# Query loads with token pairs woven for the block turn, and one decode step more at the entry of the late stage

## The chip, the cores and the metric

The kernel runs on one core of one Trainium2 chip. The time is device microseconds of one execution of the program on that core. The engines are named as the profile names them: PE (TensorE), PEld (its weight loads), DVE (VectorE), ACT (ScalarE), POOL (GpSimd) and SP (SyncE, which here issues nearly all DMAs).

## What is computed

Linear attention with random features over 4 batches, 8 heads, 576 tokens and head size 64, then two gated or plain feed-forward layers over the 2304 tokens, all in float32:

```python
def phi(x):                                   # x: q or k, scaled by 64 ** -0.25
    proj = np.einsum('bhsd,md->bhsm', x, omega)          # 128 features
    h = proj - np.sum(x * x, axis=-1, keepdims=True) / 2.0
    return np.exp(h - np.max(h, axis=-1, keepdims=True)) / np.sqrt(m)
kv = np.einsum('bhsm,bhsd->bhmd', k_p, v);  z = np.sum(k_p, axis=2)
num = np.einsum('bhsm,bhmd->bhsd', q_p, kv)
out = num / (np.einsum('bhsm,bhm->bhs', q_p, z)[..., None] + 1e-06)
# x: out as 2304 tokens x 512
xn = x / sqrt(mean(x * x) + 1e-06) * rms_g;  g = xn @ w_gate          # 512 x 1536
x = (silu(g) * (xn @ w_val)) @ w_out                                   # 1536 x 512
h = x @ w_in;  out = silu(h) @ w_out2                                  # 512 x 2048, 2048 x 512
```

The weights arrive as float64 and are decoded on the chip from their two 32-bit words.

## The kernel before

Every float32 product of the feed-forward layers is three passes over a high and a low part (`PASS`). The program has two stages.

**The attention stage** is a list of operations (`Op`), each with an engine, a duration, the operations it needs, the buffers it claims and frees. A table written out by hand, `ORDER`, gives the sequence in which all of them are emitted, and so the order on each engine; every engine runs its own list in order. `run_order` walks that table with the durations written in the `Op`s and with `LAT`, `TURN` and `LAND`, and uses the resulting clock for one thing alone: which of a resource's slots (`SLOTS`; six PSUM buffers `b`, four tiles `x`, four `e`, two `qT` and so on) an operation gets, the one that is free first by this reckoning.

A unit is 256 tokens of four heads of q or k (kinds `q`, `k`), or the 64 tokens that are left over in each of two batches (`qt`, `kt`). For a unit, SP loads a tile `x` (L530; the left-over ones L521), POOL squares it (L581), PE turns it (L632), PE projects it on the features (L661, into a PSUM buffer `b`), DVE takes maxima (L678) and ACT the exponentials `e` (L709). From k, PE adds the products with v (L739, `kv`); the left-over tokens' v lies in the tile `vat` (L521). From q, the exponentials must be turned so that the features lie on the partitions, and then PE multiplies them with `kv` (L843). That turn is done in two ways. For units 0 to 17 of a running count (`count`, `BY_DMA`) PE turns (L819) and ACT copies (L825). For the 18 others, those of the last two batches and one pair of left-over pieces, SP moves four blocks of 32 partitions from `e` to `qT` (L799, four DMAs, operation `ed`) and DVE turns 32 x 32 blocks back into `e` (L806, operation `eT`). Then DVE divides (L857 to L877), ACT, POOL and PE normalise and turn the result into `xs`, the input of the layers (L908 to L961). In the gaps PE computes the first sweep of the first layer for the first three of five blocks of tokens (L250 and L1067).

In this stage all DMAs go through SP's one list, in the order of the table: loads of q, k, v and weights, and the moves `ed`. An x load is written as

```python
nc.sync.dma_start(out=dst.rearrange("p h r d -> p h (r d)"),
    in_=src[b, heads, 256 * hf:256 * hf + 256, :].rearrange("h (p r) d -> p h (r d)", r=2))
```

so partition p holds tokens 2p and 2p+1 (`r`), 512 bytes together for each head. The turn of `e` writes its 128 tokens at every fourth element (`p h (t b) -> p b h t`).

**The late stage** begins with `run_order`'s end. A generator, `stream`, issues the remaining sweeps of both layers on PE without a gap by intent (L250 the first products `g`, L304 and L337 the second products `y`), in PSUM buffers that take over the place of the six `b`. Between them, `prep.tick` moves a pipeline of weights on by one step: it emits the decode of one weight on DVE (L154 to L165) and POOL (L168), the scale and the high part of the one before on ACT (L176, L191), the low part of the one before that on DVE (L194), and the load of one more (L142, L144). A tick is emitted whenever `due`, a count of PE time, passes 3.2 or 5.5.

Of the kernel before, what the change touches and what calls it, by code (L numbers as in the profile page):

```python
# [20 lines left out]
def kernel(  # L21
# [14 lines left out]
    nc = tc.nc  # L36
# [6 lines left out]
    G = 4  # L43
    KC = DM // P
# [61 lines left out]
    f = 0  # L106
# [4 lines left out]
    f = 0  # L111
# [121 lines left out]
    prep = Prep()  # L233
# [5 lines left out]
    W_EARLY, GRAIN, GATE = 3, 3, 3  # L239
# [155 lines left out]

    ops = []
    LAT = {"PE": 0.22, "DVE": 0.15, "ACT": 0.18, "Pool": 0.08, "SP": 0.0}
    PE_SLOW, TURN, LAND = 5.5, 0.1, 2.4
    FIRST = {"PE": 1.5, "DVE": 2.0, "ACT": 3.3, "Pool": 2.4, "SP": 0.7}


# [112 lines left out]
    va_ring = [kp.tile([P, G, 2, D + 1], F32, tag=f"va{n}", name=f"va{n}", bufs=1) for n in range(SLOTS["v"])]  # L514
    va_tail = [kp.tile([P, G, 1, D + 1], F32, tag=f"vat{n}", name=f"vat{n}", bufs=1) for n in range(2)]

    def fetch(dst, src, kind, b, hf, g, parts=range(2)):
        heads = slice(G * g, G * g + G)
        if len(kind) == 2:
            for e in parts:  # L520
                nc.sync.dma_start(  # L521
                    out=dst[64 * e:64 * e + 64, :, 0, 0:D],
                    in_=src[b + e, heads, 512:576, :].rearrange("h p d -> p h d"),
                )
        elif src is v:
            rows = src[b, heads, 256 * hf:256 * hf + 256, :].rearrange("h (p r) d -> p h r d", r=2)
            for r in range(2):
                nc.sync.dma_start(out=dst[:, :, r, 0:D], in_=rows[:, :, r, :])
        else:
            nc.sync.dma_start(  # L530
                out=dst.rearrange("p h r d -> p h (r d)"),
                in_=src[b, heads, 256 * hf:256 * hf + 256, :].rearrange(
                    "h (p r) d -> p h (r d)", r=2
                ),
            )
# [27 lines left out]
    count, BY_DMA = [0], range(18, 36)  # L563

    def add_load(u):
        kind, b, hf, g = u
        tail = len(kind) == 2
        R = 1 if tail else 2
        w = ld[u] = State()

        def emit(o):
            w.x = buf(load_p, [P, G, R, D], "x", o.slot["x"])
            fetch(w.x, k if kind[0] == "k" else q, *u)

        w.op = Op("ld_x." + kind[0], "SP", 1.2 if tail else 0.5, emit, claim=["x"], xfer=0.55 * R)

        def squares(o):
            w.sq = buf(wk, [P, G * R * D], "sq", o.slot["sq"])
            w.ns = buf(wk, [P, G * R], "ns", o.slot["ns"])
            xf = w.x.rearrange("p h r d -> p (h r d)")  # L580
            nc.gpsimd.tensor_tensor(out=w.sq, in0=xf, in1=xf, op=ALU.mult)  # L581

        def halve(n):
            sv = w.sq.rearrange("p (a d) -> p a d", d=D)
            nc.gpsimd.tensor_tensor(  # L585
                out=sv[:, :, 0:n], in0=sv[:, :, 0:n], in1=sv[:, :, n:2 * n], op=ALU.add
            )

        w.sqop = Op("sq." + kind[0], "Pool", 0.17 + 0.43 * R, squares, [w.op], ["sq", "ns"])
        h1 = Op("half1." + kind[0], "Pool", 0.17 + 0.28 * R, lambda o: halve(D // 2), [w.sqop])  # L590
        h2 = Op("half2." + kind[0], "Pool", 0.17 + 0.14 * R, lambda o: halve(D // 4), [h1])

        def norms(o):
            nc.vector.tensor_reduce(  # L594
                out=w.ns, in_=w.sq.rearrange("p (a d) -> p a d", d=D)[:, :, 0:D // 4], axis=AX.X, op=ALU.add
            )

        w.nsop = Op("norms." + kind[0], "DVE", 0.2, norms, [h2], free=[(w.sqop, "sq")])
        if kind == "k":
            z = vld[u] = State()  # L600

            def emit_v(o):
                z.v = va_ring[o.slot["v"]]
                fetch(z.v, v, *u)

            z.op = Op("ld_v", "SP", 1.0, emit_v, claim=["v"], xfer=1.7)
        return w
# [12 lines left out]
    def add_unit(u):  # L620
        kind, b, hf, g = u
        tail = len(kind) == 2
        R = 1 if tail else 2
        w = add_load(u)
        st = State()
# [68 lines left out]
            [top], free=[(w.sqop, "ns")],  # L694
        )
        res = f"et{g}" if kind == "kt" else "e"
        base = count[0]
        if kind[0] == "q":
            count[0] += R
        moved = lambda r: kind[0] == "q" and base + r in BY_DMA  # L700
        for r in range(R):

            def exps(o, r=r):
                pool = kp if kind == "kt" else wk
                blocks4 = moved(r)
                st.e[r] = buf(pool, [P, 4, G, 32] if blocks4 else [P, G, M], res, o.slot[res])
                for h in range(G):
                    src = st.ps[r][:, h, :]
                    nc.scalar.activation(  # L709
                        out=st.e[r][:, :, h, :] if blocks4 else st.e[r][:, h, :],  # L710
                        in_=src.rearrange("p (a f) -> p a f", a=4) if blocks4 else src, func=AF.Exp,
                        bias=st.nb[:, G * r + h:G * r + h + 1],
                    )

            exs.append(Op(
                "ex." + kind[0], "ACT", 1.004, exps, [nb] + exs, [res],
                [(pjs[r], "b"), (pjs[r], "pjc")] + ([(mxs[0], "nb")] if r == R - 1 else []),
            ))
        if kind[0] == "k":
            add_kv(u, st, exs)  # L720
        else:
            evs = [add_flip_e(st, r, exs[r], moved(r)) for r in range(R)]
            num = None
            for r in range(R):
                num = add_q(u, st, r, evs, num)
# [63 lines left out]
            tu, tst, tex, pad, _, vop = ktexp[b - 1, g]  # L789
            add_tail(b - 1, g, 1, tst, tex, vop, [(tex, f"et{g}"), (pad, f"vt{g}")])  # L790

    def add_flip_e(st, r, ex, by_dma):
        pe = {}
        if by_dma:

            def move(o):
                pe[0] = buf(wk, [P, G, P], "qT", o.slot["qT"])
                for a in range(4):
                    nc.sync.dma_start(  # L799
                        out=pe[0][32 * a:32 * a + 32],  # L800
                        in_=st.e[r][:, a].rearrange("p h f -> p (h f)"),
                    )

            def turn(o):
                turned = st.e[r].rearrange("p a h f -> p (a h f)").rearrange("p (h t) -> p h t", h=G)
                nc.vector.transpose(  # L806
                    out=turned.rearrange("p h (t b) -> p b h t", b=4),
                    in_=pe[0].rearrange("p b (h f) -> p b h f", h=G),
                )
                st.e[r] = turned  # L810

            mv = Op("ed", "SP", 2.1, move, [ex], ["qT"], xfer=1.5)
            tp = Op("eT", "DVE", 0.92, turn, [mv], free=[(mv, "qT")])
            return tp, (ex, "e")

        def flip(o):
            pe[0] = buf(ps_a, [P, G, P], "b", o.slot["b"])
            for h in range(G):
                nc.tensor.transpose(pe[0][:, h, :], st.e[r][:, h, :], ident)  # L819

        fl = Op("fl", "PE", 0.436, flip, [ex], ["b"], [(ex, "e")])

        def evac(o):
            st.e[r] = buf(wk, [P, G, P], "qT", o.slot["qT"])
            nc.scalar.activation(out=st.e[r], in_=pe[0], func=AF.Copy)  # L825

        ev = Op("ev", "ACT", 0.495, evac, [fl], ["qT"], [(fl, "b")])
        return ev, (ev, "qT")
# [140 lines left out]
    w_done = {}  # L969
# [26 lines left out]
    def add_block(j, fs, n):  # L996
# [4 lines left out]
        for f in fs:  # L1001
# [3 lines left out]
            def product(nm, claim, prev, f=f, st=st):  # L1005
                head = None
                for c0 in range(0, 3 * KC, GRAIN):

                    def emit(o, c0=c0):
                        if c0 == 0:  # L1010
                            st.p[nm] = buf(ps_a, [P, blocks[j]], "b", o.slot["b"])
                        part(wt[1, nm, f], j, st.p[nm], c0, c0 + GRAIN)

                    prev = Op(
                        "part", "PE", 0.227 * GRAIN, emit, xdeps + [w_done[1, nm, f], prev],
                        claim if c0 == 0 else [],
                    )
                    head = head or prev
                return head, prev
# [39 lines left out]
        for d in range(KC):  # L1059
            sy, head = State(), None  # L1060
            for f, h in zip(fs, hcl):

                def out_part(o, d=d, sy=sy, f=f):
# [6 lines left out]
                        )  # L1070

                g2 = before[f] = Op(
                    "out", "PE", 0.68, out_part, [prev, low[f], w_done[1, "o", f], before.get(f), head],
                    [] if head else ["b", "fm"], [(h, "h")] if d == KC - 1 else [],
                )
                head = head or g2
# [13 lines left out]
    with tc.manual_schedule():  # L1090
# [64 lines left out]
            n = add_block(j, sweeps[0][1], n)  # L1155
        prev = [o for o in ops if o.label in ("xf", "out")] + [xslo[t] for t in range(TB * NE, TB * NE + TB)]
        for job in prep_list(1)[:W_EARLY]:
            prev = [Op("late", "PE", 0.227 * 3 * KC, lambda o: None, [*prev, w_done[job[2]]], ["b"])]
            prev[0].free.append((prev[0], "b"))
        run_order()  # L1160
        att.close()
# [7 lines left out]
        pools["s"] = (late, 3)  # L1169
        prep.jobs += prep_list(1)[W_EARLY:]  # L1170
        due = 0.0
        for c in stream():
            due += c
            if due > (W_PACE if prep.done(1) else W_RUSH):
                prep.tick()
                due = 0.0
# [30 lines left out]
```

## Time and profile before

| | |
|---|---|
| median of 3 runs | 982.79 us (981.89 to 983.13) |
| the profiled execution | 982.64 us, of which the span from first to last instruction 980.8 us |
| PE | 973.3 us busy, 99% of the span |
| DVE, ACT, POOL | 59%, 40%, 30% of the span |
| granted TensorE clock | 0.999 of full speed |
| attention stage | about 0 to 189 us |
| late stage | about 189 us to the end |

A busy PE is to be read with care: the ends of matmuls are modelled and overlap the next start, so a short wait of PE can be missing from its idle time. The chain of work that ended last and the distances from start to start tell more. Issues on SP carry the name SPq; they are not counted as busy, and a wait of SP shows as a distance between the end of one and the start of the next.

### The profile page before, as it was taken

What the parts mean: (1) busy time and instruction counts of PE and PEld (TensorE: products, weight loads), DVE (VectorE), ACT (ScalarE), POOL (GpSimd) and SP (SyncE); (2) the same over time, 40 slices, a digit from 0 to 9 for tenths busy, and PEclk for the clock granted to TensorE, in tenths of its full rate; (3) what the DMA queues carried; (4) which work ended last, traced back from release to release, by engine and by line L of the source; (5) the groups of instructions that cost most, each with busy time, mean ns of one, the idle gap of its engine ahead of it and who ended that gap; (6) DMA issues with size and microseconds to landing.
All of it is one profiled execution on the core that took longest, in us unless ns stands there. A gap on an engine that the chain in (4) does not pass through costs nothing.

```text
span 980.8 us, 15411 instructions
## 1 busy us (share of the span) xinstructions
PE 973.3 (99%) x5938; PEld 828.3 (84%) x5938; DVE 576.1 (59%) x1186; ACT 392.2 (40%) x904; POOL 292.5 (30%) x308
## 2 busy tenths in 40 slices
PE   9999999999999999999999999999999999999998
PEld 8989888887888888888898888888888888888887
DVE  7999999778533366774234873615634734435634
ACT  7999777753311123341112334443223223222221
POOL 8877653346300033441001322402402312202200
PEclk9999999999999999999999999999999999999999
DMA  7644444223200012221000111201201201100023
GB/s 194 161 106 137 124 117 114 71 68 105 86 1 1 1 43 65 87 86 44 1 1 21 50 59 43 65 22 43 65 22 43 65 22 43 43 1 22 22 86 108
DMA packets 79481, 60.31 MB, mean 61 GB/s; under 512 B 27312, under 2 KB 73648, under 8 KB 79408
## 3 DMA queue, kind: packets, MB, share of 16 engines
q1 hardware_dynamic: 79136, 59.26, 20.6%
q8 instruction: 47, 0.77, 0.3%
q14 instruction: 26, 0.21, 0.1%
q10 hardware_dynamic: 272, 0.07, 0.0%
HBM read 49.87 MB, written 4.72 MB: 56 GB/s over the span
## 4 chain that ended last, share of the span: by engine, by line
PE 95%; DVE 2%; DMA 1%; ACT 1%; issue 1%; POOL 0%; SPq 0%; ACTq 0%; DVEq 0%
PE g L250 45%; PE y L337 20%; PE y L304 13%; PE b L661 5%; PE b L250 3%; PE kv L739 2%; PE b L843 2%; PE b L1067 2%; PE b L632 2%; DVE w L194 1%; PE b L819 1%; PE b L947 1%; DMA raw<-in_moe_w_out_dram 0%; DMA om<-in_omega_dram 0%; DVE m L154 0%
## 5 line engine op out<-in xcount | busy, mean ns | idle before, releaser
L250 PE MATMUL g<-xs,w 128*128 128x512 f32 (+1 forms) x2256 | 468.0, 366 | 0.0
L250 PEld LDWEIGHTS g<-xs,w 128*128 128x128 f32 x2256 | 391.2, 188 | 70.0
L168 POOL TENSOR_TENSOR m<-m,raw 128x512 int32<-128x512 int32 x136 | 189.4, 1393 | 579.6 <-issue 413.4
L244 DVE TENSOR_TENSOR h<-s,h 128x512 fp32r<-128x512 f32 (+1 forms) x134 | 96.0, 717 | 185.1 <-ACT h L243 185.1
L337 PE MATMUL y<-w,h 128*128 128x512 f32 (+1 forms) x870 | 200.8, 388 | 0.0
L337 PEld LDWEIGHTS y<-w,h 128*128 128x128 f32 x870 | 162.2, 188 | 33.2
L243 ACT ACTIVATE h<-s 128x512 fp32r<-128x512 f32 (+1 forms) x134 | 78.7, 588 | 182.0 <-DVE s L273 160.0
L304 PE MATMUL y<-h,w 128*128 128x512 f32 (+1 forms) x648 | 135.6, 366 | 0.6 <-DVE w L194 0.6
L304 PEld LDWEIGHTS y<-h,w 128*128 128x128 f32 x648 | 112.1, 189 | 20.8 <-DVE w L194 1.0
L284 ACT ACTIVATE s<-g 128x512 f32<-128x512 f32 (+1 forms) x80 | 44.4, 555 | 171.1 <-PE g L250 171.0
L348 DVE TENSOR_TENSOR ya<-y,ya 128x512 f32<-128x512 f32 (+1 forms) x91 | 62.1, 684 | 57.9 <-PE y L337 56.5
L315 DVE TENSOR_TENSOR ya<-y,ya 128x512 f32<-128x512 f32 (+1 forms) x80 | 50.2, 635 | 54.4 <-PE y L304 54.2
L273 DVE TENSOR_TENSOR s<-s,g 128x512 f32<-128x512 f32 (+1 forms) x54 | 33.8, 626 | 81.1 <-PE g L250 80.4
L709 ACT ACTIVATE e<-b,nb 128x128 f32<-128x128 f32 x272 | 75.6, 401 | 13.4 <-DVE nb L691 4.8
L191 ACT ACTIVATE w<-m 128x512 fp32r<-128x512 f32 x68 | 42.8, 630 | 69.4 <-POOL m L168 68.2
L661 PE MATMUL b<-bd,hl 128*128 128x256 f32 x432 | 62.1, 288 | 0.7 <-DVE xt L870 0.5
L661 PEld LDWEIGHTS b<-bd,hl 128*128 128x128 f32 x432 | 55.1, 188 | 3.7 <-ACT e L709 0.8
L194 DVE TENSOR_TENSOR w<-m,w 128x512 fp32r<-128x512 f32 x68 | 53.8, 792 | 2.8 <-ACT w L191 2.7
L678 DVE TENSOR_REDUCE small<-b 128x4 f32<-128x512 f32 x72 | 49.8, 691 | 4.7 <-PE b L661 2.7
L267 ACT ACTIVATE s<-g 128x512 f32<-128x512 f32 (+1 forms) x54 | 29.5, 546 | 57.2 <-PE g L250 57.1
L585 POOL TENSOR_TENSOR sq<-sq 128x256 f32<-128x256 f32 (+2 forms) x80 | 45.8, 584 | 2.4
L581 POOL TENSOR_TENSOR sq<-x 128x512 f32<-128x512 f32 (+1 forms) x40 | 38.3, 963 | 26.7 <-DVE ns L594 10.9
(75 smaller groups left out, 728.0 us busy)
## 6 DMA issues: line engine op xcount, KB each, us to landing
raw<-in_moe_w_out_dram SPq DMA_DIRECT2D x28, 512.0 KB, 3.5
raw<-in_moe_w_in_dram SPq DMA_DIRECT2D x16, 512.0 KB, 3.7
raw<-in_moe_w_gate_dram SPq DMA_DIRECT2D x12, 512.0 KB, 3.6
raw<-in_moe_w_val_dram SPq DMA_DIRECT2D x12, 512.0 KB, 3.5
qT<-e SPq DMA_DIRECT2D x72, 64.0 KB, 2.2
x<-in_k_dram SPq DMA_DIRECT2D x16, 256.0 KB, 3.5
va<-in_v_dram SPq DMA_DIRECT2D x32, 128.0 KB, 3.8
x<-in_q_dram SPq DMA_DIRECT2D x16, 256.0 KB, 3.6
```

Source lines behind the costliest of these rows:

```text
L168: tt(out=mi, in0=mi, in1=(low if step == 5 else high).bitcast(I32), op=ALU.add)
L194: nc.vector.tensor_tensor(out=st.t[:, 1, :], in0=st.m.bitcast(F32), in1=st.t[:, 0, :].bitcast(F32), op=ALU.subtract)
L243: nc.scalar.activation(out=ht[:, 0, :], in_=s, func=AF.Copy)
L244: nc.vector.tensor_tensor(out=ht[:, 1, :], in0=s, in1=ht[:, 0, :].bitcast(F32), op=ALU.subtract)
L250: nc.tensor.matmul(out=ps, lhsT=w[:, a, cc * P:(cc + 1) * P], rhs=xs[j][:, c, cc, :], start=(n == 0), stop=(n == 3 * KC - 1),)
L304: nc.tensor.matmul(out=ps, lhsT=wt[1, "o", f][:, a, d * P:(d + 1) * P], rhs=hs[f][:, c, :], start=(n == 0), stop=(n == nn - 1),)
L315: nc.vector.tensor_tensor(out=y[:, d, :], in0=ps, in1=y[:, d, :], op=ALU.add)
L337: nc.tensor.matmul(out=ps, lhsT=hs[f][:, a, t * P:(t + 1) * P], rhs=wt[2, "p", f][:, c, d0:d1], start=(n == 0), stop=(n == nn - 1),)
L348: nc.vector.tensor_tensor(out=o[:, t, d0:d1], in0=ps, in1=o[:, t, d0:d1], op=ALU.add)
L661: nc.tensor.matmul(out=st.ps[r][:, 2 * j:2 * j + 2, :].rearrange("p h m -> p (h m)"), lhsT=st.hl[:, c, 2 * r + j, :], rhs=bd[:, a, :], sta ...
L678: nc.vector.tensor_reduce(out=st.mx[:, G * r:G * r + G], in_=st.ps[r], axis=AX.X, op=ALU.max)
L709: nc.scalar.activation(out=st.e[r][:, :, h, :] if blocks4 else st.e[r][:, h, :], in_=src.rearrange("p (a f) -> p a f", a=4) if blocks4 els ...
```

## The change

Four parts. First, the x load of a two-token q unit whose exponentials go by `ed` and `eT` is made by four DMAs instead of one, one for each head, with another order of tokens on the partitions: partition 4t+c gets the pair t of the 32-pair group c. These are the eight q units of the last two batches. Second, for these the turn `eT` writes its tokens next to each other instead of at every fourth element; the tokens come out in the same places as before. Third, durations in the reckoning that chooses slots are changed (`TURN`, the x load, `eT`, `part`, `out`, `late`); `ORDER` itself is not. Fourth, `prep.tick()` is called once before the first product of the late stage.

```diff
-    PE_SLOW, TURN, LAND = 5.5, 0.1, 2.4
+    PE_SLOW, TURN, LAND = 5.5, 0.12, 2.4
...
+        elif woven:
+            for h in range(G):
+                nc.sync.dma_start(
+                    out=dst[:, h].rearrange("p r d -> p (r d)"),
+                    in_=src[b, G * g + h, 256 * hf:256 * hf + 256, :].rearrange(
+                        "(c t r) d -> t c (r d)", c=4, r=2
+                    ),
+                )
...
+        if kind[0] == "q":
+            w.moved = count[0] in BY_DMA
+            count[0] += R
+        w.woven = w.moved and not tail
...
-        w.op = Op("ld_x." + kind[0], "SP", 1.2 if tail else 0.5, emit, claim=["x"], xfer=0.55 * R)
+        w.op = Op("ld_x." + kind[0], "SP", 2.1 if w.woven else 1.2 if tail else 0.5, emit, claim=["x"], xfer=0.55 * R)
...
-                    out=turned.rearrange("p h (t b) -> p b h t", b=4),
+                    out=turned.rearrange("p h (b t) -> p b h t" if w.woven else "p h (t b) -> p b h t", b=4),
...
-            tp = Op("eT", "DVE", 0.92, turn, [mv], free=[(mv, "qT")])
+            tp = Op("eT", "DVE", 0.65 if w.woven else 0.92, turn, [mv], free=[(mv, "qT")])
...
-                        "part", "PE", 0.227 * GRAIN, emit, xdeps + [w_done[1, nm, f], prev],
+                        "part", "PE", 0.235 * GRAIN, emit, xdeps + [w_done[1, nm, f], prev],
...
-                    "out", "PE", 0.68, out_part, [prev, low[f], w_done[1, "o", f], before.get(f), head],
+                    "out", "PE", 0.72, out_part, [prev, low[f], w_done[1, "o", f], before.get(f), head],
...
-            prev = [Op("late", "PE", 0.227 * 3 * KC, lambda o: None, [*prev, w_done[job[2]]], ["b"])]
+            prev = [Op("late", "PE", 0.23 * 3 * KC, lambda o: None, [*prev, w_done[job[2]]], ["b"])]
...
         due = 0.0
+        prep.tick()
         for c in stream():
```

The order of PE and POOL is the same in both programs. SP's list is the same but for the loads. This is SP from the moves that run from 107 us on, before (x is the tile of a load, qT and e those of a move, va and vat hold v, raw a weight):

```order
L799 DMA qT_2368<-e_2245 32x4x128 x4
L530 DMA x_2412<-in_q_dram 128x4x128
L530 DMA x_2462<-in_q_dram 128x4x128
L521 DMA vat_102<-in_v_dram 64x4x64
L530 DMA x_2522<-in_q_dram 128x4x128
L142 DMA raw_2535<-in_moe_w_out_dram 128x1024
L799 DMA qT_2569<-e_2503 32x4x128 x4
L530 DMA x_2580<-in_q_dram 128x4x128
L799 DMA qT_2603<-e_2513 32x4x128 x4
L528 DMA va_101<-in_v_dram 128x4x64 x2
L530 DMA x_2713<-in_q_dram 128x4x128
L521 DMA vat_103<-in_v_dram 64x4x64
```

Between the v load and the last x load stand two more DMAs of a left-over q unit, the same in both. The same stretch after:

```order
L808 DMA qT_2377<-e_2254 32x4x128 x4
L531 DMA x_2421<-in_q_dram 128x1x128 x4
L531 DMA x_2474<-in_q_dram 128x1x128 x4
L521 DMA vat_102<-in_v_dram 64x4x64
L531 DMA x_2537<-in_q_dram 128x1x128 x4
L142 DMA raw_2553<-in_moe_w_out_dram 128x1024
L808 DMA qT_2587<-e_2518 32x4x128 x4
L531 DMA x_2598<-in_q_dram 128x1x128 x4
L808 DMA qT_2624<-e_2528 32x4x128 x4
L528 DMA va_101<-in_v_dram 128x4x64 x2
L531 DMA x_2734<-in_q_dram 128x1x128 x4
L521 DMA vat_103<-in_v_dram 64x4x64
```

Five loads of one DMA have become five of four; the two `vat` loads stand behind two and behind all five of them.

At the first products of the late stage PE's instructions are the same, but the PSUM place that a product takes over is another, and with it the engine that it waits for. Before (g is the PSUM tile of one product of 12 matmuls, w0_2 the weight of the second, and the brackets name the engine whose work is waited for):

```order
L1067 MATMUL b3_3533<-h1_3425,w0_5_2888 128x512 x3
L250 MATMUL g_3576<-xs3_93,w0_0_1047 128x512 x10
L250 MATMUL g_3591<-xs3_93,w0_2_1803 128x512 [waits PE_49]
L250 MATMUL g_3591<-xs3_93,w0_2_1803 128x512 x11
L250 MATMUL g_3625<-xs3_93,w0_3_2311 128x512 [waits Activation_49]
```

After:

```order
L1076 MATMUL b2_3557<-h1_3449,w0_5_2912 128x512 x3
L250 MATMUL g_3602<-xs3_93,w0_0_1047 128x512 x10
L250 MATMUL g_3617<-xs3_93,w0_2_1809 128x512 [waits Activation_49]
L250 MATMUL g_3617<-xs3_93,w0_2_1809 128x512 x11
L250 MATMUL g_3644<-xs3_93,w0_1_1907 128x512 [waits PE_49]
```

The last product of the attention stage has moved from `b3` to `b2`, and the second product of the late stage now waits for ACT, which copies such buffers out (L1079), where it waited for PE alone.

On DVE the extra tick puts a decode of five instructions ahead of the first two `s` and `h` of the late stage. After:

```order
L970 TENSOR_TENSOR xs_94<-b_3571,xs_94 128x4x128
L154 TENSOR_SCALAR m_3618<-raw_3600 128x512
L157 TENSOR_SCALAR raw_3600<-raw_3600 128x512
L160 TENSOR_SCALAR m_3618<-m_3618 128x512
L162 TENSOR_SCALAR raw_3600<-raw_3600 128x512
L165 TENSOR_SCALAR m_3618<-m_3618 128x512
L273 TENSOR_TENSOR s<-s,g 128x512
L244 TENSOR_TENSOR h<-s,h 128x512
```

Before, that decode stood behind the first `s` and `h`:

```order
L961 TENSOR_TENSOR xs_94<-b_3547,xs_94 128x4x128
L273 TENSOR_TENSOR s<-s,g 128x512
L244 TENSOR_TENSOR h<-s,h 128x512
L154 TENSOR_SCALAR m_3626<-raw_3592 128x512
L157 TENSOR_SCALAR raw_3592<-raw_3592 128x512
```

The weights that follow move up by one place with it, and the two orders are the same again further on in the next sweep.

## Rows read from the trace of the kernel before

**Rows 1.** The page: span, and each engine's busy time, share and instructions.

```profile
span 980.8 us, 15411 instructions
...
PE 973.3 (99%) x5938; PEld 828.3 (84%) x5938; DVE 576.1 (59%) x1186; ACT 392.2 (40%) x904; POOL 292.5 (30%) x308
```

**Rows 2.** Busy time by stretch: us; PE, PEld, DVE, ACT, POOL (instructions); clock; DMA.

```profile
96.00:189.00 93.00, 92.80 (x938) 79.37 (x937) 86.73 (x213) 69.44 (x189) 49.63 (x67) 1.00 0.36 102
189.00:236.00 47.00, 46.44 (x239) 39.46 (x239) 34.56 (x60) 24.18 (x51) 21.63 (x16) 1.00 0.29 91
```

**Rows 3.** The chain that ended last, 108 to 114 us: start, us, what.

```profile
108.41 1.11 DVE e L806
...
112.08 1.89 PE b L250 x7
```

**Rows 4.** Timeline of SP, 107 to 131 us: start, us, what.

```profile
107.56 5.15 SPq L799 DMA_DIRECT2D qT<-e  x8
112.81 1.09 SPq L530 DMA_DIRECT2D x<-in_q_dram  x2
113.95 0.66 SPq L521 DMA_DIRECT2D vat<-in_v_dram  x1
116.86 0.37 SPq L530 DMA_DIRECT2D x<-in_q_dram  x1
117.28 1.62 SPq L142 DMA_DIRECT2D raw<-in_moe_w_out_dram  x1
120.16 2.51 SPq L799 DMA_DIRECT2D qT<-e  x4
122.77 0.53 SPq L530 DMA_DIRECT2D x<-in_q_dram  x1
123.41 2.49 SPq L799 DMA_DIRECT2D qT<-e  x4
125.94 2.02 SPq L528 DMA_DIRECT2D va<-in_v_dram  x2
128.07 1.36 SPq L521 DMA_DIRECT2D x<-in_q_dram  x2
129.54 0.54 SPq L530 DMA_DIRECT2D x<-in_q_dram  x1
130.12 0.60 SPq L521 DMA_DIRECT2D vat<-in_v_dram  x1
```

**Rows 5.** Timeline of PE: the two products with the left-over tokens' v.

```profile
119.08 0.64 PE L739 MATMUL kv<-vat,et 128*64 128x65 f32 x16
...
134.15 0.64 PE L739 MATMUL kv<-vat,et 128*64 128x65 f32 x16
```

**Rows 6.** Issue time of DMAs by line, whole run: ns min/median/max, first and last start.

```profile
L530 SPq DMA_DIRECT2D x<-in_q_dram x16: 367/429/549, 6.4 to 129.5; - x16
...
L799 SPq DMA_DIRECT2D qT<-e x72: 547/600/1492, 96.0 to 178.6; - x72
...
L521 SPq DMA_DIRECT2D x<-in_q_dram x8: 595/612/662, 43.0 to 132.3; - x8
```

**Rows 7.** The tile vat: time from issue to landing of its eight loads.

```profile
DMA to landing us min/median/max: 3.0/3.6/4.3
```

**Rows 8.** Groups of DVE, 95 to 189 us: busy us, mean ns, idle before.

```profile
L806 DVE STREAM_TRANSPOSE e<-qT 128x512 f32<-128x512 f32 x18 | 19.6, 1098 | 1.2 <-DMA qT<-e 1.1
...
L649 DVE TENSOR_TENSOR hl<-b,hl 128x512 fp32r<-128x512 f32 (+1 forms) x12 | 7.7, 639 | 0.6 <-ACT hl L645 0.6
```

**Rows 9.** Entry of the late stage: first products on PE, last copies of the stage before on ACT.

```profile
188.73 14.01 PE L250 MATMUL g<-xs,w 128*128 128x512 f32 x72
...
191.27 1.07 ACT L1079 ACTIVATE ya<-b 128x512 f32<-128x512 f32 x2
```

**Rows 10.** The last wait of PE: the low part of a weight, and PE after it.

```profile
233.55 1.79 DVE L194 TENSOR_TENSOR w<-m,w 128x512 fp32r<-128x512 f32 x1
...
235.39 6.68 PE L304 MATMUL y<-h,w 128*128 128x512 f32 x28 [0.56 <-DVE w L194]
```

More of the change, by code (lines that the diff above doesn't have):

```diff
@@ L515, with fetch @@
     va_tail = [kp.tile([P, G, 1, D + 1], F32, tag=f"vat{n}", name=f"vat{n}", bufs=1) for n in range(2)]
-    def fetch(dst, src, kind, b, hf, g, parts=range(2)):
+    def fetch(dst, src, kind, b, hf, g, parts=range(2), woven=False):
         heads = slice(G * g, G * g + G)
@@ L569, in add_load @@
         w = ld[u] = State()
+        w.moved = False
+        if kind[0] == "q":
+            w.moved = count[0] in BY_DMA
+            count[0] += R
+        w.woven = w.moved and not tail
         def emit(o):
             w.x = buf(load_p, [P, G, R, D], "x", o.slot["x"])
-            fetch(w.x, k if kind[0] == "k" else q, *u)
-        w.op = Op("ld_x." + kind[0], "SP", 1.2 if tail else 0.5, emit, claim=["x"], xfer=0.55 * R)
+            fetch(w.x, k if kind[0] == "k" else q, *u, woven=w.woven)
+        w.op = Op("ld_x." + kind[0], "SP", 2.1 if w.woven else 1.2 if tail else 0.5, emit, claim=["x"], xfer=0.55 * R)
         def squares(o):
@@ L696, in add_unit @@
         res = f"et{g}" if kind == "kt" else "e"
[L697 to L700, printed above, removed]
         for r in range(R):
@@ L704, in exps @@
                 pool = kp if kind == "kt" else wk
-                blocks4 = moved(r)
+                blocks4 = w.moved
                 st.e[r] = buf(pool, [P, 4, G, 32] if blocks4 else [P, G, M], res, o.slot[res])
@@ L721, in add_unit @@
         else:
-            evs = [add_flip_e(st, r, exs[r], moved(r)) for r in range(R)]
+            evs = [add_flip_e(st, r, exs[r], w) for r in range(R)]
             num = None
@@ L790, in add_kv, with add_flip_e @@
             add_tail(b - 1, g, 1, tst, tex, vop, [(tex, f"et{g}"), (pad, f"vt{g}")])
-    def add_flip_e(st, r, ex, by_dma):
+    def add_flip_e(st, r, ex, w):
         pe = {}
-        if by_dma:
+        if w.moved:
             def move(o):
```

## The prediction

> **What bounds the kernel now.** I read the page first: PE is busy 973.3 of 980.8 us [rows 1]. The busy time by stretch says the same of the two stretches that the change touches, with a granted clock of 1.00: in 93.0 us of the attention stage PE is idle for 0.2, in 47.0 us after its end for 0.56 [rows 2]. DVE is the next engine, busy 86.73 of the 93.0. So whatever PE has to wait for is added to the time, and little can be taken away: of the chain that ended last, the turn on DVE is only one link, once, from 108.41 to the matmul at 112.08 [rows 3], and the one clear wait later is the 0.56 us before the matmul at 235.39 [rows 10]. Then I read SP's list, since three of the loads' DMAs are new there, and asked for each instruction behind them who needs it and when.
>
> SP is nearly full where five of the eight woven loads lie. From 107.56 us one issue follows another. Up to the second `vat` load at 130.12 there are two real pauses, 114.61 to 116.86 (a tile `x` is still read by PE) and 118.90 to 120.16 (the exponentials are not ready), 3.5 us together [rows 4]. The two `vat` loads, the left-over tokens' v, are needed soon after: a `vat` lands 3.0 to 4.3 us after its issue, 3.6 in the median [rows 7], so those of 113.95 and 130.12 land at about 117.55 and 133.72, and PE multiplies with them at 119.08 and 134.15 [rows 5]. That leaves 1.5 and 0.4 us.
>
> **The change part by part.**
>
> *The turn.* A `STREAM_TRANSPOSE` takes 1098 ns; a plain DVE pass over as many elements with one read from PSUM takes 639 [rows 8]. No row shows one with contiguous output. Bounds: no gain, and 1098 - 639, about 0.46 us each, 7.4 us of DVE for the sixteen. I take 0.4 from the nearness of the plain pass. This is DVE's time, not PE's. On PE it can give back what hangs on the turn: some 0.4 at 112.08 [rows 3], and perhaps 0.2 in the last turns before 189, where PE's whole idle time is 0.2 [rows 2]. The first is lost again if PE then waits at 119.08 for a load, so I count 0.2.
>
> The Trainium skill (SBUF — State Buffer, the note on cachelines ahead of the worked example) speaks for this part: accesses that stay within a 16-byte line go at full rate, those that move to a new line each time pay. A turn with every fourth float32 writes a new line each time. By the page the turn should get faster; no run here shows by how much, and the sum hardly changes.
>
> *The loads.* A q load of one DMA costs SP 0.57 us from its start to the next (two from 112.81 to 113.95). How long one of the four new ones takes is not in the trace. Bounds: 0.43 us, the median of the one-DMA loads (with the 0.04 us that the moves pause between two, 0.47), and 0.64, the moves' distance (5.15 us for eight) [rows 4, 6]; the loads of 64 partitions take 0.61. I take 0.64: like the moves, the new loads carry 64 KB in 128 pieces of 512 bytes, their source is not one even step per partition as in the quick loads, and the built program marks the quick ones, and not these, the moves and the 64-partition loads, as prepared ahead. Four cost 2.58, so each woven load adds 2.0 us to SP. The first three, before 96 us, stand ahead of pauses and cost nothing.
>
> At the first `vat`, two woven loads are ahead: issue at 112.81 + 8 x 0.644 = 117.96, landing at 121.56, PE waits from 119.08: 2.5 us. From there SP has work without a pause, because what it paused for is ready before it comes: the tile at 116.86, and the exponentials at 120.16 plus at most those 2.5. From the end of the first `vat` issue, 118.67: three woven loads 7.73, weight 1.67, moves 2.61 and 2.53, v 2.13, left-over q 1.47 [rows 4]; 18.14 together, so the second `vat` would go out at 136.81. Two of these hold long issues (1.62 for a weight; 2.02 for two of v, where 1.0 is usual); whether they recur at the same places is open, and I take half of their 2.1 us: 135.77, landing at 139.4. PE wanted it at 134.15: **5.2 us later in all**, the 2.5 included. With both long issues 6.3. With neither and a landing of 3.0, 3.6. With 0.47 per issue twenty issues take 3.5 less. After 134 the moves have up to 5 us in hand, since PE is late too, and SP, with no more woven loads, catches up.
>
> *The slots.* PE's order is unchanged, but the second product of the late stage now takes over a PSUM buffer that ACT empties. The two last copies end at 192.34 (191.27 + 1.07); the product starts twelve matmuls after 188.73, at 0.24 each about 191.6 [rows 9, 10]. If it is the last copy, PE waits **0.8**; if the one before, 0.2. I take 0.8: the order names the last product's own buffer. Elsewhere in the attention stage slots move too; those waits, if any, end before the second `vat` lands and are inside the 5.2.
>
> *The extra tick.* It adds no work: five decode instructions, at 0.64 us or less each [rows 8] some 3 us, move ahead of an `s` that must wait for PE's second product, 24 matmuls or 5.8 us after 188.73, anyway. The decode whose low part ended at 235.34 now comes one tick earlier, two such products or about 5.5 us, so the wait of 0.56 goes: **-0.6** [rows 10]. If the crowd of weights at the entry makes an `h` late instead, this comes back; bounds 0 and -0.6.
>
> Sum: +5.2 + 0.8 - 0.6 - 0.2 = +5.2. The profiled execution took 982.64 us, 0.15 below the median, so 987.8, and as a median **987.9 us**.
>
> **The rivals.** A change within 0.2%, 2 us, is what a measurement of this kernel can hardly tell from none.
>
> *Quick issues (0.12).* If the new loads issue as the one-DMA loads do, SP is 3.5 us less late: 1.7 in place of 5.2, 984.4; without the long issues about 983.4. For it: both fill 128 partitions. Against it: every other kind of 64 KB DMA takes 0.6.
>
> *No wait for v (0.10).* SP takes the three extra issues without a delay that reaches PE; what remains is 0.8 - 0.6 - 0.6 = -0.4, 982.4, or without the wait for ACT 981.6. That needs an issue of about 0.2 us: five loads then add some 1.2 us and the pauses swallow it. No issue of a load took less than 0.367. [...]
>
> *DVE was the hidden bound (0.04): faster.* In the 93 us DVE is 93% busy, and modelled matmul ends hide short waits. If a third of the freed 7.4 us were on PE's path, the time would be 980.3. It decides only if SP's loads cost PE nothing as well. Against it: one link in the chain.
>
> *The clock (0.04): above 991.* [...]
>
> **How the numbers follow.** The forecast, `vat` late by the slow issue, has 0.70 and spans 985 to 991 (3.6 to 6.3 from the loads, 0.2 to 0.8 from the copy, 0 to -0.6 from the tick, and some room above for a wait that no row shows). The range 983.0 to 991.0 adds the quick issues and leaves out no wait for v, the faster case and the clock, 0.18 together. Faster by over 0.2%: 0.04. Within 0.2%: the case without a wait and most of the quick one, 0.20. Slower: 0.76.
>
> **What would show it.** Right: new q loads near 0.6 us each on SP, no pause there from 107 to 137 us; PE idle before the two `vat` products, some 2 and 3 us, ended by that DMA; a turn of 0.7 us; no wait of PE near 235; one of 0.8 at the second product of the late stage, ended by ACT. Wrong: loads of 0.4 us or less, or `vat` products that start without a wait.

## The result, and the profile after

The changed kernel takes **988.65 us** (median of 6 runs, 987.49 to 990.20), the kernel before 983.19 (6 runs, 981.89 to 983.51): a ratio of 1.0060, 95% interval 1.0049 to 1.0071. It is slower by 5.5 us. The profiled execution took 988.99 us, its span is 987.1, 6.3 more than the span of [rows 1].

The timeline of SP after (start, us, what) answers to [rows 4]:

```profile
107.44 5.15 SPq L808 DMA_DIRECT2D qT<-e  x8
112.69 6.45 SPq L531 DMA_DIRECT2D x<-in_q_dram  x8
119.17 0.62 SPq L521 DMA_DIRECT2D vat<-in_v_dram  x1
119.91 2.49 SPq L531 DMA_DIRECT2D x<-in_q_dram  x4
122.44 0.59 SPq L142 DMA_DIRECT2D raw<-in_moe_w_out_dram  x1
123.14 2.56 SPq L808 DMA_DIRECT2D qT<-e  x4
125.80 2.53 SPq L531 DMA_DIRECT2D x<-in_q_dram  x4
128.44 2.56 SPq L808 DMA_DIRECT2D qT<-e  x4
131.04 2.39 SPq L528 DMA_DIRECT2D va<-in_v_dram  x2
133.55 1.36 SPq L521 DMA_DIRECT2D x<-in_q_dram  x2
135.01 2.51 SPq L531 DMA_DIRECT2D x<-in_q_dram  x4
137.56 0.62 SPq L521 DMA_DIRECT2D vat<-in_v_dram  x1
```

Each row starts 0.03 to 0.12 us after the one above it ends: both pauses of [rows 4] are gone. The four DMAs of a woven load (L531) take 2.5 us where one load took 0.5, and the two `vat` go out at 119.17 and 137.56, 5.2 and 7.4 us later than before. From issue to landing the first took 2.4 us and the second 2.3, where the two of the kernel before took 3.3 and 3.1. These two alone, after and before:

```profile
L521 SPq DMA_DIRECT2D vat<-in_v_dram x2: 623/624/624, 119.2 to 137.6; - x2
...
DMA to landing us min/median/max: 2.3/2.4/2.4
```

```profile
L521 SPq DMA_DIRECT2D vat<-in_v_dram x2: 602/632/662, 113.9 to 130.1; - x2
...
DMA to landing us min/median/max: 3.1/3.2/3.3
```

So the two `vat` land sooner after their issue than before; what is late is the issue.

The timeline of PE around the two products with `vat`, against [rows 5]; the bracket is the idle time before a row and what ended it:

```profile
121.73 0.69 PE L748 MATMUL kv<-vat,et 128*64 128x65 f32 x16 [3.13 <-DMA vat<-in_v_dram]
122.35 2.60 PE L674 MATMUL b<-bd,hl 128*128 128x256 f32 x12
124.74 1.05 PE L645 MATMUL b<-ident,x 128*128 128x128 f32 x4
...
140.03 0.69 PE L748 MATMUL kv<-vat,et 128*64 128x65 f32 x16 [1.40 <-DMA vat<-in_v_dram]
...
194.54 3.02 PE L250 MATMUL g<-xs,w 128*128 128x512 f32 x12
198.20 11.29 PE L250 MATMUL g<-xs,w 128*128 128x512 f32 x60 [0.64 <-ACT ya L1088]
209.32 5.64 PE L304 MATMUL y<-h,w 128*128 128x512 f32 x24
...
220.39 0.63 PE L304 MATMUL y<-h,w 128*128 128x256 f32 x4
221.22 2.66 PE L304 MATMUL y<-h,w 128*128 128x256 f32 x20 [0.20 <-DVE h L244]
223.72 16.51 PE L250 MATMUL g<-xs,w 128*128 128x512 f32 x72
```

PE is 2.65 us later at the first product (121.73 against 119.08), 5.88 at the second (140.03 against 134.15), and enters the late stage 5.81 later (194.54 against 188.73). At that entry the second product waits for ACT; [rows 9] have all 72 matmuls without a break.

### The profile page after: what moved, and what is told of

Its sections match the earlier page's. It is cut to its first block, busy times and chain, and to the rows that moved or that the text cites. A ratio compares the mean times of both kernels' runs of the same rounds, so it can differ in the third digit from the quotient of the medians.

```text
span 987.1 us, 15433 instructions
## 1 busy us (share of the span) xinstructions
PE 975.2 (99%) x5938; PEld 830.1 (84%) x5938; DVE 570.9 (58%) x1186; ACT 392.6 (40%) x904; POOL 291.3 (30%) x308
## 4 chain that ended last, share of the span: by engine, by line
PE 92%; DMA 2%; ACT 1%; POOL 1%; SPq 1%; DVE 1%; issue 0%; ACTq 0%; DVEq 0%; POOLq 0%
PE g L250 46%; PE y L337 20%; PE y L304 13%; PE b L674 4%; PE b L250 2%; PE kv L748 2%; PE b L852 1%; PE b L1076 1%; PE b L645 1%; SPq L531 1%; PE b L828 1%; DMA va<-in_v_dram 1%; PE b L956 1%; DMA vat<-in_v_dram 0%; POOL sq L598 0%
```

## The experiments

All twelve kernels are set against the kernel before on the same chip, whose median was 982.8 to 983.1 us.

**1. The changed kernel again (`after_again`), unaltered.**

> The changed kernel once more, unaltered, for a second profile. All theories: 987.4 to 990. In the first profile the granted clock was 0.50 from 123.2 to 124.8 us, right after PE's wait of 3.13 us, and PE still waited 1.40 us for the second vat. If the lateness of SP alone sets the end, a profile without that fall shows a second wait longer by about 1.5 us and the same time. If the fall of the clock is in the end time, the time without it is lower by about 1.5 us.

988.41 us (987.79 to 989.79), ratio 1.0053 (1.0037 to 1.0070). The granted clock fell again in the profiled execution. The same stretches of PE in both profiles (us; PE; clock; DMA share; GB/s), first of the first profile after, then of this one:

```profile
119.00:124.00 5.00, 2.27 (x25) 0.88 0.41 97
124.00:130.00 6.00, 6.00 (x33) 0.82 0.61 183
```

```profile
119.00:124.00 5.00, 2.27 (x41) 0.94 0.31 85
124.00:130.00 6.00, 6.00 (x31) 0.76 0.67 179
```

Here PE waited 2.73 and 1.39 us. A profile of this kernel without a fall, which would have told the cases apart, didn't come up. The mean clock of each execution says a little (see the clock below).

**2. Both vat loads earlier (`vat_both_early`).** In the list of the order, 479 and 617 are the `vat` loads, 769, 895 and 856 woven loads.

```diff
-        715, 639, 810, 1124, 593, 1125, 640, 716, 811, 643, 1126, 1127, 1128, 731, 641, 682, 478,
+        715, 639, 810, 1124, 593, 1125, 640, 716, 811, 643, 1126, 1127, 1128, 731, 641, 682, 478, 479,
-        770, 814, 771, 772, 735, 757, 758, 759, 736, 720, 684, 685, 895, 688, 479, 721, 815, 816,
-        773, 1119, 760, 1058, 762, 761, 737, 616, 689, 686, 738, 722, 763, 687, 856, 764, 774, 1131,
+        770, 814, 771, 772, 735, 757, 758, 759, 736, 720, 684, 685, 895, 688, 721, 815, 816,
+        773, 1119, 760, 1058, 762, 761, 737, 616, 689, 686, 738, 722, 763, 687, 856, 617, 764, 774, 1131,
-        745, 1132, 1068, 617, 749, 825, 826, 596, 746, 836, 783, 837, 896, 695, 832, 784, 1069, 838,
+        745, 1132, 1068, 749, 825, 826, 596, 746, 836, 783, 837, 896, 695, 832, 784, 1069, 838,
```

> The changed kernel with its two vat loads moved ahead in SP's order, the first in front of the pair of woven loads, the second behind the third one; as many issues as before. Theory A, as the prediction has it (only vat is late, what stands behind it has slack): both waits for vat go and the time is 988.65 - 5.8 = 982.9. Theory B (SP as such is late, by 10 us more of issues less 4 to 5 us of pauses): both waits for vat go, but the moves that went out at 134.1 in the kernel before go out at about 139, their turns start 5 us later, and PE needs them at 144.3 where they had 0.6 us to spare: PE waits 3 to 4 us by 145, and the time is 986 to 987.5. Rival, the buffers and the clock and not the loads: no change, 988.65.

987.86 us (986.62 to 988.08), ratio 1.0047 (1.0032 to 1.0062). Theory A, 982.9, is out; the time lies 0.4 us above the range of theory B, and PE waits earlier than B said. From the changed kernel's 988.41 the intervals don't tell it, so this run alone doesn't rule out the rival that the loads aren't the cause; runs 5 and 8 do. Its PE timeline:

```profile
128.94 1.66 PE L250 MATMUL b<-xs,w 128*128 128x512 f32 x6 [0.95 <-DVE xt L879]
...
136.17 1.15 PE L852 MATMUL b<-kvs,e 128*64 128x65 f32 x32 [1.54 <-DVE e L815]
...
138.06 0.67 PE L748 MATMUL kv<-vat,et 128*64 128x65 f32 x16
```

Neither `vat` is waited for, and PE is still 3.9 us late at the second (138.06 against 134.15). Its chain shows how, through what SP issues behind the woven loads, here a weight:

```profile
123.02 4.41 DMA raw<-in_moe_w_out_dram
127.46 0.43 DVE m L154
```

DVE runs its list in order: behind the decode of the late weight (L154) stand the pass `xt` and the rest, down to the turn at 135.41 for which PE waits. Kept from one consumer, the lateness here reached PE through the next.

**3. Only the first vat load earlier (`vat_first_early`).** The edit is the part of run 2 that moves 479.

> The changed kernel with only the first vat load moved ahead, in front of the pair of woven loads. If SP's lateness is one sum that ends at the second vat: no wait near 119, one wait of 5 to 6 us near 134 to 140, and a time within 1 us of 988.65. If each wait costs by itself: 988.65 - 2.65 = 986.0. If a wait of that length lets the clock fall and PE then has no further wait to hide it: 1.5 to 2 us above 988.65.

988.63 us (988.48 to 988.83), ratio 1.0058 (1.0043 to 1.0073): one sum that ends at the second `vat`.

```profile
139.57 0.69 PE L748 MATMUL kv<-vat,et 128*64 128x65 f32 x16 [1.51 <-DMA vat<-in_v_dram]
```

The rest of the lateness comes as three other waits (0.37, 1.53, 1.68), not as the one long wait expected. The clock stayed at 1.00 from 119 to 152 us, and the time is that of the changed kernel. PE gets to the second `vat` as late with a fall of the clock as here without one (140.03 and 139.57), as it would if SP alone set that time.

**4. The split alone (`split_only`).** The kernel before, with this in `fetch` for the same eight loads:

```diff
+        elif split:
+            for h in range(G):
+                nc.sync.dma_start(
+                    out=dst[:, h].rearrange("p r d -> p (r d)"),
+                    in_=src[b, G * g + h, 256 * hf:256 * hf + 256, :].rearrange("(p r) d -> p (r d)", r=2),
+                )
```

> The kernel before with the same eight q loads issued as four DMAs, one per head, of the same rows in the old token order: turn, buffers and decode steps as before. If the number of issues is the cost, at 0.62 us each: 5.1 to 5.9 us over the kernel before, 988.3 to 989.1, with the same two waits for vat. If only the woven form is slow and a plain quarter issues as a one-DMA load does (0.37 to 0.47): 1.0 to 1.7 us over it, 984.2 to 984.9. If the loads are not the cause: 983.2.

985.05 us (984.14 to 985.86, 10 runs), ratio 1.0021 (1.0012 to 1.0030): the second case, a little above its bound. The issue time by line (ns min/median/max, first and last start), after and here:

```profile
L531 SPq DMA_DIRECT2D x<-in_q_dram x32: 542/602/1919, 68.1 to 136.9; - x32
...
DMA to landing us min/median/max: 2.1/2.3/4.8
```

```profile
L531 SPq DMA_DIRECT2D x<-in_q_dram x32: 341/430/1917, 68.0 to 132.8; - x32
...
DMA to landing us min/median/max: 1.9/2.3/4.2
```

As many DMAs of 64 KB in 128 pieces, landing as soon (2.3 us in the median), but an issue of 0.43 us each in place of 0.60. The woven source takes two steps from partition to partition, the plain one a single step, and the built program marks the plain quarters, not the woven ones, as prepared ahead. Which of the two makes the difference isn't shown; the single step alone doesn't, since the left-over loads of 64 partitions have it, lack the mark and take 0.61 [rows 6]. The waits for `vat` shrink to 1.02 and 0.47. So the time has two parts: four issues instead of one cost 2.0 us. The further 3.4 us to the changed kernel (988.41 in run 1) go with the form and the other edits. By the rows of runs 6 and 9 the moved buffer and the decode step add some 0.5, which leaves 2.9 for the form; by run 5 all other edits together, the turns too, take 0.6 off, which makes it 4.0.

**5. The turn without the weave (`turn_no_weave`).** The loads are one DMA each; the queries of the eight units come out in another order.

```diff
-            fetch(w.x, k if kind[0] == "k" else q, *u, woven=w.woven)
+            fetch(w.x, k if kind[0] == "k" else q, *u)
```

> The changed kernel with its eight q loads as one DMA each, as before: the turn writes contiguous tokens, buffers and decode step are the changed ones, and the queries of those units come out in another order than the reference's. Theory of SP: no wait for vat, no late load: 983.0 + 0.65 (the wait for ACT's copy at the second product of the late stage) + 0.2 (the new wait before a y product near 221) - 0.56 (the wait near 235) - 0.25 (the faster turn at 112) = 983.0. If DVE was a hidden bound, the turns' 6.4 us of DVE give back a third: 981. If something else than the loads makes the changed kernel slow: 987 to 988.4.

982.57 us (981.86 to 984.82, 11 runs), ratio 0.9995 (0.9987 to 1.0004). Take the woven loads away, and the slowdown is gone, with the turns at their new length (mean 744 ns over the 18, two of which are the left-over tokens' old ones) and the other two edits in place.

**6. Without the extra decode step (`no_tick`).**

```diff
         due = 0.0
-        prep.tick()
```

> The changed kernel without the extra decode step. The prediction's term: the wait of 0.56 us before a y product near 240 comes back, and the wait of 0.20 near 221 goes if it is the tick's: 988.4 + 0.56 - 0.20 = 988.8. If the step changes nothing that PE waits for: 988.4. If the earlier decodes at the entry cost more than they give: under 988.

989.25 us (988.08 to 990.62, 5 runs), ratio 1.0061 (1.0047 to 1.0075), too near the changed kernel's to be told from it. The rows decide: the wait near 221 is gone, and the old one is back:

```profile
221.53 3.04 PE L304 MATMUL y<-h,w 128*128 128x256 f32 x24
224.40 16.51 PE L250 MATMUL g<-xs,w 128*128 128x512 f32 x72
...
243.27 2.11 PE L304 MATMUL y<-h,w 128*128 128x512 f32 x8 [0.55 <-DVE w L194]
```

**7. The planner's numbers alone (`slots_only`).** The kernel before with the changed durations, as in the change's diff, and nothing else of it.

> The kernel before with only the changed planner's numbers, which move PSUM and SBUF buffers about; no woven load, the old turn, no extra decode step. The prediction's term: PE waits for ACT's last copy at the second product of the late stage, 0.64 us as in the changed kernel: 983.0 + 0.65 = 983.7. If the buffers cost nothing here because ACT is not as late as in the changed kernel: 983.0. If other moved buffers make PE wait in the attention stage: 984.5 or more.

983.67 us (983.12 to 984.71, 11 runs), ratio 1.0006 (0.9997 to 1.0015): the first case in the size, though the interval takes in no change. The rows decide again; the wait is there without any late load:

```profile
188.73 3.02 PE L250 MATMUL g<-xs,w 128*128 128x512 f32 x12
192.41 11.28 PE L250 MATMUL g<-xs,w 128*128 128x512 f32 x60 [0.66 <-ACT ya L1084]
203.53 5.64 PE L304 MATMUL y<-h,w 128*128 128x512 f32 x24
```

From the first product to the first `y` it is 203.53 - 188.73 = 14.80 us.

**8. Three woven loads (`weave_three`).** Only those that SP issues before 96 us.

```diff
-        w.woven = w.moved and not tail
+        w.woven = w.moved and not tail and count[0] <= 24
```

> The changed kernel with only the first three q loads woven, those that SP issues before 96 us; the other five are one DMA each with the old turn. Theory of SP: the twelve issues before 96 us stand ahead of pauses and cost nothing: no wait for vat, 983.0 (+0.65 for ACT's copy, +0.2 near 221, -0.56 near 235, -0.25 for the turn at 112). If each woven load costs its share wherever it stands: 3/8 of 5.5 us, 985.1.

982.86 us (982.56 to 983.97, 11 runs), ratio 1.0000 (0.9991 to 1.0009): the three cost nothing where SP has pauses. The price is one of place.

**9. The decode step alone (`tick_only`).** The line of run 6, added to the kernel before.

> The kernel before with only the extra decode step. The prediction's term: the wait of 0.56 us before a y product near 235 goes, a wait of 0.20 near 214 comes: 983.1 - 0.36 = 982.7. If the five decode instructions at the entry make an h late: 983.3 or more.

982.72 us (982.26 to 984.00, 11 runs), ratio 1.0001 (0.9992 to 1.0010): nothing measurable. The rows around it:

```profile
189.90 14.01 PE L250 MATMUL g<-xs,w 128*128 128x512 f32 x72
203.75 5.63 PE L304 MATMUL y<-h,w 128*128 128x512 f32 x24
...
215.77 2.66 PE L304 MATMUL y<-h,w 128*128 128x256 f32 x20 [0.34 <-DVE h L244]
...
234.62 8.32 PE L304 MATMUL y<-h,w 128*128 128x512 f32 x36
```

The wait before the 36 matmuls is gone and a new one stands before the 20. From the first product to the first `y` it is 203.75 - 189.90 = 13.85 us, so the moved buffer of run 7 costs 14.80 - 13.85 = 0.95.

**10. Three woven loads with the old planner's numbers (`weave_three_old_slots`).** Run 8, with every duration of the kernel before.

> Only the first three q loads woven, the extra decode step, and the planner's numbers of the kernel before, so that the second product of the late stage takes a buffer of PE again. If the terms add up: weave_three less 0.64, so 982.2 to 982.4, below the kernel before by 0.25 + 0.36 or some 0.6, with no wait of PE for ACT near 192. If the copy of ACT is waited for in another place: 982.9, as weave_three.

**981.52 us** (981.15 to 982.26, 11 runs), ratio 0.9988 (0.9979 to 0.9997): faster than both kernels, if only by 1.3 us, and 0.7 us below what the terms gave. In its rows the 72 matmuls are in one piece again, from 188.42 us on, 14.01 us.

**11. Half of the woven loads from ACT (`woven_act_half`).**

```diff
-                nc.sync.dma_start(
+                (nc.sync, nc.scalar)[h // 2].dma_start(
                     out=dst[:, h].rearrange("p r d -> p (r d)"),
```

> The changed kernel with half of the DMAs of each woven load issued by ACT, two heads each by SP and ACT. If SP's issues are the cost: SP has 1.25 us per woven load in place of 2.5, five loads add some 3.4 us to it, the pauses of 3.5 to 5 us take that, and the waits for vat are under 0.5 each: 983 to 984.2. If the transfers themselves are slow (the pieces of 512 bytes, the landing), not the issuing: 987 to 988.5, as the changed kernel. If ACT, behind its own issues and the wait for a free tile, makes the exponentials late: 985 to 987, with PE waiting for ACT or for moves that wait for ACT.

986.65 us (985.93 to 988.09, 4 runs), ratio 1.0040 (1.0026 to 1.0053), as the third case. There is no wait for `vat` any more, which are issued at 116.68 and 133.75 and land after 2.5 and 2.4 us, as in the changed kernel: so it was SP's issuing and not the transfers. But ACT issues the same DMAs no faster, between its exponentials: 0.60 us in the median, as SP's part of them.

PE waits 0.73 us for ACT's `qT` at 84.34 and 0.45 for DVE at 101.02, and enters the late stage at 191.89, 3.2 after [rows 9]. How much of the 3.2 is ACT's, and how much SP's remaining issues', these rows don't separate.

**12. Three woven loads and nothing else (`weave_three_alone`).** Run 10 without the line of run 6.

> The kernel before with the first three q loads woven and their six turns contiguous, and nothing else of the change: old planner's numbers, no extra decode step. It splits the 1.3 us that the two together gained. If the turn gives what the chain showed, one link of 0.25 to 0.4: 982.5 to 982.7, with the wait of 0.56 near 235. If the turns give most of the 1.3 because DVE limits the attention stage beyond that link: 981.5 to 982.0. If the gain was the step's alone or chance: 982.9.

981.99 us (981.32 to 983.26, 11 runs), ratio 0.9991 (0.9982 to 1.0000), at the edge of what can be told: most of the 1.3 us goes with the three woven loads and their six turns, the second case, though the intervals don't shut out the others.

## Why the prediction was right, and where its terms were off

**The path through SP** was right. New loads of 0.64 us: 0.60 in the median, 0.63 from one to the next (2.49 for four, and a gap). No pause from 107 to 138: so it was. PE waits of 2.5 and 2.7 more at the two products: the shifts are 2.65 and 5.88, against 2.5 and 5.2 in all. That these come so near is in part luck, because two errors cancel. SP was later than forecast: the `vat` went out at 119.17 and 137.56, forecast were 117.96 and 135.77, and 136.81 with both long issues. Long issues did come, one of 1.92 us among the eight woven loads at 112.69, where none was counted, and 2.39 for the two v at 131.04; that of the weight did not (0.59 at 122.44). Against this a `vat` landed in 2.4 and 2.3 us, where the prediction took 3.6 and had 3.0 as its bound. With 3.6, PE would have come to the second product at about 141.2 (137.56 + 3.6), 7.0 us late, outside the 3.6 to 6.3 of this term. Why they landed sooner the runs don't show.

Runs 5 and 8 show that the loads are the cause. That it is their issue show run 4, where as many transfers land as soon (2.3 us in the median) and cost less with a shorter issue, and run 11, where the waits for `vat` go when SP has fewer issues.

In the profiles the parts add up: 5.81 later at the entry of the late stage, 0.93 for the moved buffer, 0.43 less for the decode step (both below), 6.3 together, as the spans differ. The medians differ by 5.5; the profiled execution before was 0.5 below its median, the one after 0.3 above.

**What the prediction didn't see** is that `vat` is only where SP's lateness is met first. It had the moves "up to 5 us in hand, since PE is late too"; that holds only while PE is late. Freed of both `vat` (run 2), PE meets late weights, passes and turns, and gets back 0.6 us of the 5.5 at most, a difference within the noise. The five loads add some 10 us of issuing to a stretch with 3.5 us of pauses, and what is over reached PE, in runs 2 and 3 in part by other ways than `vat`.

**The form of the DMA** carried more of the time than its number. The quick rival's price for the loads, +1.7, is about what run 4 measured (+2.0). It was the right price for a split that keeps the step and the mark of the quick loads, and the choice of the slow one rested on that difference. (The prediction's floor for an issue, 0.367 us, is that of the x loads; weight loads of line 142 took 0.327 at least and 0.340 in the median, still far above the 0.2 that "no wait for v" needs.)

**The moved buffer:** 0.8 forecast, 0.93 to 0.95 measured: 209.32 - 194.54 = 14.78 us after, 13.85 where the buffer is PE's own. The wait shown is shorter, 0.64: the modelled ends hide a part, so distances between starts are the safer reading.

**The decode step:** the wait near 235 went, as forecast, but the step is not free. A wait before a `y` product (221.22 after) takes its place. From that `y` to the next product it is 3.33 us (220.39 to 223.72) with the step and 2.87 without, in run 6 (221.53 to 224.40): 0.46 lost. What the old wait cost is again more than its 0.56; the 36 matmuls of that `y` in the kernel before, then after:

```profile
232.86 1.98 PE L304 MATMUL y<-h,w 128*128 128x512 f32 x8
...
241.91 16.48 PE L250 MATMUL g<-xs,w 128*128 128x512 f32 x72
```

```profile
240.07 8.32 PE L304 MATMUL y<-h,w 128*128 128x512 f32 x36
248.23 1.98 PE L250 MATMUL g<-xs,w 128*128 128x512 f32 x8
```

To the next product it was 9.05 us and is 8.16, 0.89 gained. Some 0.4 us are left, and run 9 can't tell that from nothing. The prediction named an `h` made late as a bound; it is what happens, in part.

**The turn:** 1098 to 701 ns, the 0.4 us that were taken. By the Trainium skill (SBUF — State Buffer, the note on cachelines) each access that crosses to a new line pays; the trace agrees in direction. For PE the prediction had 0.2 us. The times of run 12, and of run 5 less its other edits, rather give 1 us, so this term may be too small. The profiles don't settle it. Of the 0.7 us by which PE is ahead at 188 in run 12 (188.03), 0.6 arise at 64 us, before the first woven load, in a wait that is 0.89 us in the kernel before, 0.27 here and 0.26 to 0.90 in the other profiles; no turn stands ahead of it.

**The clock:** it fell, though the rival had 0.04, and the time stayed below 991. Since PE had to wait for the second `vat` anyway, the fall need not have cost anything; that it didn't isn't shown. Of the ten executions of the changed kernel (the result and run 1), the five with a mean clock of 0.998 took 988.07 to 990.20 us, 988.99 in the median, the five at 1.000 took 987.49 to 988.89, 987.79 in the median. These ranges overlap, and a later SP could bring both the fall and the longer time.

## What to carry to other kernels

Before a load is split, add up the issues in the stretch where its queue has the fewest pauses, not over the whole run: the same edit cost nothing before 96 us and 5.5 us after 107. Look at the form too: here plain quarters, which the built program marks as prepared ahead, issued in 0.43 us, and woven quarters, moves and 64-partition loads, which it doesn't mark, in 0.60. When a queue is short of time, moving the one load that is waited for may only show the next one, as in run 2; take issues away or put the split where pauses are.

## What was not expected of the hardware

After the wait of 3.13 us for the first `vat` the granted clock went from 1.00 to 0.50, the lower of its two levels (1.2 and 2.4 GHz), and it was at 1.00 again from 126.4 us on (the profile after; us, PE, clock, DMA share, GB/s):

```profile
121.70:123.20 1.50, 1.47 (x21) 0.86 0.33 97
123.20:124.80 1.60, 1.60 (x10) 0.50 0.63 134
124.80:126.40 1.60, 1.60 (x8) 0.56 0.97 345
126.40:128.00 1.60, 1.60 (x9) 1.00 0.52 116
```

Twelve matmuls took 2.39 us here (122.35 to the next row at 124.74), and 1.53 in the kernel before (119.65 to 121.18):

```profile
119.65 1.70 PE L661 MATMUL b<-bd,hl 128*128 128x256 f32 x12
121.18 0.60 PE L632 MATMUL b<-ident,x 128*128 128x128 f32 x4
```

The fall came after waits of 2.73 and 3.13 us; in run 3, with waits of 1.51 to 1.68, it didn't.
